# Starting the FFN on two batches of four in a fused retention and SwGLU kernel, and moving the next chunk's attention by a slot or two

## Chip, cores, metric

One core of one Trainium2 chip. The metric is the device time of one execution in microseconds (us). Several executions are timed for each kernel, the kernel before and the changed one in turn on the same chip. An execution is marked fast or slow; on one core "slow" only means that it took over 1.5% longer than the fastest of the same kernel.

## The reference

```python
# retention: q, k, v are (4 batches, 8 heads, 768 steps, 64)
state = gamma[None, :, None, None] * state + np.einsum('bhd,bhe->bhde', k[:, :, t], v[:, :, t])
y[:, :, t] = scale * np.einsum('bhd,bhde->bhe', q[:, :, t], state)
# then, on x = y as (4 * 768 tokens, 512):
xn = x / np.sqrt(np.mean(x * x, axis=-1, keepdims=True) + 1e-06) * rms_g
g = xn @ w_gate                                   # 512 x 1536
out = (g * (1.0 / (1.0 + np.exp(-g))) * (xn @ w_val)) @ w_out
```

All inputs and the output are float32; the kernel multiplies in bf16.

## The kernel before

It works in 6 chunks of 128 steps. The FFN of chunk c is a list of slots on TensorE: 12 for gate and value (one of 12 column blocks each, `gv`), then the output products (`down`). Pieces of the attention of chunk c+1, and the loads and transposes of chunk c+2, are hung onto these slots by number. I call the pieces of one batch V (v times decay), T (transposes of q and k), A (scores), Y (output, state update, sum of squares), R (rstd, one over the root of the mean square), N (norm) and X (transpose of the normed tile, giving xnT), S the first state; L is a load of q, k and v by GpSimd's queue. Chunks 0 and 1 transpose on TensorE; chunks 2 to 5 transpose by DMA, issued from SyncE's queue. In profile lines xn is a normed tile and xt_ps its transpose on TensorE, qT and kT are the transposed q and k, a_ps the scores, am the scores times decay or mask, g_ps and v_ps gate and value, hT their product, o_ps the output, and hot the zero tile of the filler.

```python
    # ahead of the FFN: H = filler matmuls on a zero tile, G and U = loads of gate and value weights
    for step in ("H9 H8 C0 T0 H4 V0 A0 H4 V1 T1 H4 G0 Y0 R0 U0 H4 A1 V2 T2 H4 Y1 R1 G1 U1 H2 A2 N0 T3 Y2 R2 "
                 "X0 N1 H2 A3 X1 N2 H9 H6 X2 H3 V3 Y3 H6 G2 U2 R3 N3").split():
        P[step[0]](0, int(step[1]))
    # ... cut: piece_t
        if c > 1:
            for n in "qk":
                t = work.tile([128, NHP, 128], BF16, name=n + "T", bufs=8)
                nc.sync.dma_start_transpose(out=t, in_=d[n + "b"])
                d[n + "T"] = t
            return
    # ... cut: in which slot of FFN c a piece of chunk c+1 stands, by batch
    PLAN = dict(a=(5, 5, 9, 9), y=(7, 8, 11, 12), n=(9, 10, 13, 13))
    PLAN1 = dict(v=(7, 9, 11, 14), t=(8, 10, 12, 15), a=(9, 11, 14, 17), y=(10, 13, 16, 19), n=(12, 15, 18, 21), x=(13, 17, 20, 22))
    # ... cut: loads (L) and transposes (T) for chunk c+2 (with -1: chunk c+1), W = output weights
    AHEAD = {1: ((L, 0),), 3: ((L, 1),), 5: ((L, 2),), 7: ((T, 0),), 8: ((T, 1),), 9: ((L, 3),), 11: ((T, 2),), ...}
    AHEAD0 = {2: ((L, -1, 1),), 4: ((W, 0),), 5: ((L, -1, 2),), 6: ((W, 1),), 8: ((L, -1, 3),), 9: ((W, 2), (L, 0)),
              11: ((L, 1),), 13: ((T, 0),), 14: ((L, 2),), 15: ((T, 1),), 19: ((T, 2), (L, 3))}
    LATE0 = {0: ((V, 0), (V, 1), (V, 2)), 1: ((T, 3),), 4: ((V, 3),)}    # in FFN 1, for chunk 2
```

## Time and profile before

| | before |
|---|---|
| time, median of the first 3 executions | 237.87 us (237.45 to 238.83) |
| span of the profiled execution | 236.0 us |
| TensorE (PE) busy | 226.4 us, 96% |
| mean granted PE clock | 0.998 |
| first FFN matmul | 20.43 us |

PE is full from 20.43 us on but for waits of 1.86 us in all. The lines that show this are in the prediction. Two more views also belong here, and I had not asked for either. The first is SyncE's queue between 45 and 95 us, here the rows around the DMA transposes of chunk 2, batches 2 and 3 (start, time in the queue, what):

```profile
58.81 1.19 SPq L183 DMA_TRANSPOSE qT<-qb  x1
60.52 1.19 SPq L183 DMA_TRANSPOSE kT<-kb  x1
61.81 1.52 SPq L381 DMA_DIRECT2D out_dram<-o_sb  x3
...
65.78 1.74 SPq L183 DMA_TRANSPOSE qT<-qb  x1
67.72 1.19 SPq L183 DMA_TRANSPOSE kT<-kb  x1
```

The rows at 58.81 and 60.52 are batch 2's, ahead of the output stores; those at 65.78 and 67.72 are batch 3's. The trace has batch 3's k landing at 67.70 and its kT at 74.72. PE wants kT near 81: the kernel before is 6.3 us ahead here.

The second is the DMA view of the stretch from 68 to 92 us:

```profile
DMA packets 14356, 3.96 MB, mean 165 GB/s; under 512 B 13851, under 2 KB 13851, under 8 KB 14354
q0 software_dynamic: 8653, 2.12, 113.6%
q1 hardware_dynamic: 5701, 1.81, 56.4%
```

q0 is GpSimd's queue (the loads), q1 SyncE's and ScalarE's (transposes, stores); the last figure of a row is the time that its packets took, over 16 engines' time; packets overlap, so it can pass 100%.

### The profile page before, as it was taken

Reading aid. Unit: us, or ns where it says so; the run is one execution under the profiler, and the core shown is the slowest. Engines: PE = TensorE matmul, PEld = TensorE weight load, DVE = VectorE, ACT = ScalarE, POOL = GpSimd, SP = SyncE. Lnnn points to the kernel's source line nnn. Section 1 sums busy time; section 2 is a strip of 40 time slices with the busy share of each in tenths; the row PEclk is TensorE's granted clock in tenths of the full one; section 3 lists DMA queues with packets and bytes.
Section 4 is the critical chain, followed back from the end, with each engine's and each line's share of the span. In section 5 each row is a group of like instructions: output and inputs, shape, how many; then the busy total and the mean of one; then the engine's idle time right before and its main releaser. Section 6 shows DMA issues by size and latency. Waiting matters only on the chain.

```text
span 236.0 us, 4231 instructions
## 1 busy us (share of the span) xinstructions
PE 226.4 (96%) x1587; PEld 119.3 (51%) x1613; DVE 126.8 (54%) x212; ACT 88.9 (38%) x172; POOL 128.5 (54%) x198
## 2 busy tenths in 40 slices
PE   7979999999899999999999999999999999999994
PEld 4657744565345555445554445554445554444443
DVE  6585435678337794147794147794148582243300
ACT  7475544432433423333433333433332532433221
POOL 8978989887997458970458970559300202000000
PEclk9999999999999999999999999999999999999999
DMA  7999999999999998899099999695900025200022
GB/s 135 178 188 204 211 193 204 206 196 139 180 271 174 163 139 152 172 213 161 11 127 122 173 205 104 79 133 135 181 0 0 3 44 152 73 0 0 0 89 90
DMA packets 87956, 30.69 MB, mean 130 GB/s; under 512 B 78528, under 2 KB 83392, under 8 KB 87936
## 3 DMA queue, kind: packets, MB, share of 16 engines
q0 software_dynamic: 54432, 16.78, 70.9%
q1 hardware_dynamic: 32832, 13.51, 30.7%
q8 instruction: 12, 0.20, 0.4%
q10 hardware_dynamic: 672, 0.13, 0.3%
q14 instruction: 8, 0.07, 0.1%
HBM read 28.58 MB, written 6.29 MB: 148 GB/s over the span
## 4 chain that ended last, share of the span: by engine, by line
PE 85%; DVE 4%; ACT 4%; POOL 3%; issue 2%; ACTq 0%; DVEq 0%; POOLq 0%
PE g_ps L340 26%; PE v_ps L340 26%; PE o_ps L375 21%; PE a_ps L208 3%; PE y_ps L226 2%; PE hot_ps L401 2%; PE y_ps L231 2%; PE kv_ps L257 2%; DVE am L214 1%; DVE xn L286 1%; PE o_ps L365 1%; ACT xsq L241 1%; DVE x L237 1%; PE xt_ps L296 1%; POOL rstd L274 1%
## 5 line engine op out<-in xcount | busy, mean ns | idle before, releaser
L344 DVE TENSOR_TENSOR hT<-sg,v_ps 128x512 bf16<-128x512 bf16 (+1 forms) x73 | 49.5, 678 | 79.9 <-PE v_ps L340 70.0
L340 PE MATMUL v_ps<-xnT,wv_b 128*128 128x512 bf16 (+2 forms) x298 | 73.5, 368 | 0.4
L340 PE MATMUL g_ps<-xnT,wg_b 128*128 128x512 bf16 (+2 forms) x293 | 73.1, 368 | 0.5
L343 ACT ACTIVATE sg<-g_ps 128x512 bf16<-128x512 f32 (+1 forms) x73 | 43.0, 589 | 64.8 <-PE g_ps L340 62.4
L375 PE MATMUL o_ps<-wo_b,hT 128*128 128x512 bf16 x267 | 61.9, 379 | 0.5 <-issue 0.2
L340 PEld LDWEIGHTS <-wv_b 128*128 128x128 bf16 x304 | 29.1, 98 | 33.1
L340 PEld LDWEIGHTS <-wg_b 128*128 128x128 bf16 x304 | 27.7, 98 | 29.2 <-DVE xnT L302 0.4
L375 PEld LDWEIGHTS <-hT 128*128 128x128 bf16 x276 | 26.1, 98 | 28.7 <-DVE hT L344 0.2
L271 POOL TENSOR_SCALAR ms<-ssq 128x1 f32<-128x1 f32 x24 | 5.6, 232 | 62.3 <-ACT xsq L241 61.9
L241 ACT ACTIVATE xsq<-x 128x512 f32<-128x512 f32 x20 | 12.6, 630 | 35.1 <-DVE x L237 33.3
L214 DVE TENSOR_TENSOR am<-a_ps,causal 128x512 bf16<-128x512 f32 x40 | 24.9, 679 | 0.0
L380 ACT COPY o_sb<-o_ps 128x512 f32<-128x512 f32 x23 | 13.2, 581 | 29.3 <-PE o_ps L375 23.3
L69 POOL DMA_DIRECT2D qb<-in_q_dram x23 | 21.7, 944 | 0.4 <-DMA kb<-in_k_dram 0.3
L175 POOL TENSOR_TENSOR vp<-v_f,vdec 128x512 bf16<-128x512 f32 x21 | 21.5, 1042 | 0.5
L74 POOL DMA_DIRECT2D v_f<-in_v_dram x23 | 21.3, 924 | 0.1
L69 POOL DMA_DIRECT2D kb<-in_k_dram x23 | 20.7, 901 | 0.1
L267 POOL CAST st_b<-st_f 64x256 bf16<-64x256 f32 x40 | 18.1, 454 | 1.3
L237 DVE TENSOR_TENSOR x<-y_ps,ydec 128x512 f32<-128x512 f32 x20 | 13.7, 684 | 2.9 <-PE y_ps L231 2.9
L282 DVE SCALAR_TENSOR_TENSOR xn<-x,rstd,g_bc 128x512 bf16<-128x512 f32 x16 | 12.7, 791 | 3.5 <-POOL rstd L274 3.5
L274 POOL TENSOR_TENSOR rstd<-ms,mhalf 128x1 f32<-128x1 f32 x24 | 13.3, 555 | 2.0
L401 PE MATMUL hot_ps<-hot 128*128 128x256 bf16 x65 | 11.6, 329 | 1.1 <-DVE hot L93 1.1
L226 PEld LDWEIGHTS <-am 128*128 128x128 bf16 x192 | 8.8, 98 | 5.3 <-DVE am L214 0.9
(71 smaller groups left out, 145.5 us busy)
## 6 DMA issues: line engine op xcount, KB each, us to landing
v_f<-in_v_dram POOLq DMA_DIRECT2D x23, 256.0 KB, 7.3
out_dram<-o_sb SPq DMA_DIRECT2D x23, 256.0 KB, 2.3
qb<-in_q_dram POOLq DMA_DIRECT2D x23, 128.0 KB, 7.1
kb<-in_k_dram POOLq DMA_DIRECT2D x23, 128.0 KB, 6.8
wo_b<-in_moe_w_out_dram POOLq DMA_DIRECT2D x3, 512.0 KB, 9.7
wg_b<-in_moe_w_gate_dram POOLq DMA_DIRECT2D x2, 384.0 KB, 6.5
wv_b<-in_moe_w_val_dram POOLq DMA_DIRECT2D x2, 384.0 KB, 7.3
wg_b<-in_moe_w_gate_dram POOLq DMA_DIRECT2D x1, 768.0 KB, 8.6
```

The source lines that it names most:

```text
L69: nc.gpsimd.dma_start(out=x.rearrange("p (h d) -> p h d", h=H), in_=src[b].rearrange("h (c p) d -> c p h d", p=C)[c])
L74: nc.gpsimd.dma_start(out=d["v_f"], in_=v[b].rearrange("h (c p) d -> c p h d", p=C)[c])
L175: (nc.vector if c == 0 and b < 3 else nc.gpsimd).tensor_tensor(out=d["vp"], in0=d["v_f"], in1=vdec[:, c, :, None].to_broadcast([128, H, D] ...
L214: nc.vector.tensor_tensor(out=am[:, i], in0=a_ps[i], in1=mask, op=ALU.mult)
L237: nc.vector.tensor_tensor(out=x, in0=y_ps, in1=ydec[:, c, :, None].to_broadcast([128, H, D]), op=ALU.mult)
L267: nc.gpsimd.tensor_copy(st_b[b][r, :, i * 64:i * 64 + 64], st_f[b][r, :, i * 64:i * 64 + 64])
L274: nc.gpsimd.tensor_tensor(out=rstd, in0=ms, in1=mhalf, op=ALU.pow)
L340: nc.tensor.matmul(ps[:, n - n0, :], w_b[:, s, n * 128:(n + 1) * 128], xnT[:, s, t], start=s == 0, stop=s == KS - 1)
L343: nc.scalar.activation(sg, g_ps, AF.Silu)
L344: nc.vector.tensor_tensor(out=hT[:, n0:n1, t], in0=sg, in1=v_ps, op=ALU.mult)
L375: nc.tensor.matmul(o_ps, hT[:, n, b * C:(b + 1) * C], wo_b[:, n, :], start=n == 0, stop=n == NFF - 1)
L401: nc.tensor.matmul(hot_ps, hot[:, 0:128], hot, start=True, stop=True)
```

## The change

Its intent: the FFN begins when two batches are ready instead of three, and the first weights are loaded ahead of the fourth batch, so less filler is run. The fourth batch's attention and the third's X go into the first slots. Chunk 1's pieces move one or two slots later, each batch's T ahead of the previous batch's Y and N, and X of its batch 3 goes into FFN 1.

```diff
-    WB = ((0, 384), (384, 768), (768, DFF))
+    WB = tuple((i * 384, (i + 1) * 384) for i in range(4))
-    PLAN1 = dict(v=(7, 9, 11, 14), t=(8, 10, 12, 15), a=(9, 11, 14, 17), y=(10, 13, 16, 19), n=(12, 15, 18, 21), x=(13, 17, 20, 22))
+    PLAN1 = dict(v=(9, 10, 13, 16), t=(9, 11, 13, 16), a=(10, 12, 15, 18), y=(11, 14, 17, 20),
+                 n=(13, 16, 19, 22), x=(15, 18, 21, None))
-        for b in range(B):
-            for n, slot in plan.items():
-                s[slot[b]].append(lambda f=pieces[n], b=b: f(c, b))
+        for n, slot in plan.items():
+            for b in range(B):
+                if slot[b] is not None:
+                    s[slot[b]].append(lambda f=pieces[n], b=b: f(c, b))
 (cut: gv takes a piece to run between its gate and value halves; load takes the names of what to load; of chunk 0's X
 only batch 0's is evicted by ScalarE, the others by VectorE; S casts its state as well, and its call moves into `first`;
 Y of chunk 0's batch 3 takes another PSUM pool; V of batch 3 stands last ahead of the FFN)
+        def first(i):                      # slots of FFN 0
+            two, three, third, fourth = slice(0, 2 * C), slice(0, 3 * C), slice(2 * C, 3 * C), slice(3 * C, GT)
+            if i == 0:
+                gv(0, 2, two, lambda: piece_x(0, 2))
+                gv(2, 3, two)
+                gv(0, 3, third)
+            elif i < 8:
+                gv(i + 2, t=three)
+            else:
+                gv(*((0, 4), (4, 8), (8, 10), (11, 12))[i - 8], fourth if i < 11 else slice(0, GT))
+                if i == 10:
+                    gv(10)
+            for f, *x in {1: ((piece_s, 0),), 2: ((piece_t, 0, 3), (piece_s, 1)), 3: ((piece_a, 0, 3),),
+                          4: ((piece_s, 2), (piece_y, 0, 3), (piece_rstd, 0, 3)), 5: ((piece_n, 0, 3), (piece_s, 3)),
+                          6: ((piece_x, 0, 3),)}.get(i, ()):
+                f(*x)
+        def second(n):                     # first two slots of FFN 1
+            gv(n, t=slice(0, GT - C))
+            if n == 0:
+                piece_x(1, B - 1)
+            else:
+                gv(0, 2, slice(GT - C, GT))
-    for step in (... "X0 N1 H2 A3 X1 N2 H9 H6 X2 H3 V3 Y3 H6 G2 U2 R3 N3").split():
+    for step in ("H9 H8 C0 T0 H4 V0 A0 H4 V1 T1 H4 G0 U0 Y0 G1 U1 R0 H4 A1 V2 T2 H4 q3 Y1 R1 k3 H2 A2 H6 N0 Y2 R2 v3 "
+                 "H2 X0 N1 H3 X1 N2 H6 G2 U2 G3 U3").split():
-    AHEAD0 = {2: ((L, -1, 1),), 4: ((W, 0),), 5: ((L, -1, 2),), 6: ((W, 1),), 8: ((L, -1, 3),), 9: ((W, 2), (L, 0)),
-              11: ((L, 1),), 13: ((T, 0),), 14: ((L, 2),), 15: ((T, 1),), 19: ((T, 2), (L, 3))}
+    AHEAD0 = {3: ((L, -1, 1),), 5: ((W, 0),), 6: ((L, -1, 2),), 8: ((W, 1),), 9: ((L, -1, 3),),
+              10: ((W, 2), (L, 0)), 12: ((L, 1),), 13: ((T, 0),), 15: ((T, 1),), 16: ((L, 2),), 20: ((L, 3),), 23: ((T, 2),)}
```

More of the change, by code (lines that the diff above doesn't have):

```diff
@@ L63, in load_first, with load @@
             raw[name] = x
-    def load(c, b):
+    def load(c, b, parts="qkv"):
         d = cur.setdefault((c, b), {})
-        for name, src in (("qb", q), ("kb", k)):
-            x = work.tile([128, DM], BF16, name=name, bufs=8)
-            nc.gpsimd.dma_start(
-                out=x.rearrange("p (h d) -> p h d", h=H),
-                in_=src[b].rearrange("h (c p) d -> c p h d", p=C)[c])
-            d[name] = x
-        d["v_f"] = loads.tile([128, H, D], F32, name="v_f")
-        nc.gpsimd.dma_start(out=d["v_f"], in_=v[b].rearrange("h (c p) d -> c p h d", p=C)[c])
+        for n in parts:
+            if n == "v":
+                x = d["v_f"] = loads.tile([128, H, D], F32, name="v_f")
+            else:
+                d[n + "b"] = work.tile([128, DM], BF16, name=n + "b", bufs=8)
+                x = d[n + "b"].rearrange("p (h d) -> p h d", h=H)
+            nc.gpsimd.dma_start(out=x, in_=dict(q=q, k=k, v=v)[n][b].rearrange("h (c p) d -> c p h d", p=C)[c])
     cur = {}
@@ L122 @@
     make_identity(nc, ident)
-    for b in range(1, B):
+    for b in (1, 2):
         load(0, b)
@@ L218, in piece_y @@
         d = cur[c, b]
-        pool, tag = (fps, "ff") if c == 0 else (aps, "at")
+        pool, tag = (fps, "ff") if c == 0 and b < B - 1 else (aps, "at")
         y_ps = pool.tile([128, H, D], F32, name="y_ps", tag=tag)
@@ L262, in piece_s @@
         nc.scalar.copy(st_f[b], piece_kv(0, b))
+        piece_sb(b)
     def piece_sb(b):
@@ L297, in piece_x @@
         xnT = cur[c, "xnT"][:, :, b * C:(b + 1) * C]
-        if c == 0 and b < 2:
+        if (c, b) == (0, 0):
             for s in range(KS):
@@ L329, in ffn, with gv @@
         slots = []
-        def gv(n0, n1=None, t=slice(0, GT)):
+        def gv(n0, n1=None, t=slice(0, GT), between=None):
             n1 = n0 + 1 if n1 is None else n1
@@ L337, in gv @@
             for ps, w_b in ((g_ps, wg_b), (v_ps, wv_b)):
+                if between is not None and ps is v_ps:
+                    between()
                 for n in range(n0, n1):
@@ L344, in gv @@
             nc.vector.tensor_tensor(out=hT[:, n0:n1, t], in0=sg, in1=v_ps, op=ALU.mult)
-        EARLY = 4
-        early = slice(0, GT - C)
-        def gv_first(n):
-            gv(n, t=early)
-            if n == 1:
-                piece_x(0, B - 1)
-            if n == EARLY - 1:
-                gv(0, EARLY, slice(GT - C, GT))
+        def first(i):
[18 more added lines that the diff above has]
+                piece_x(1, B - 1)
+            else:
+                gv(0, 2, slice(GT - C, GT))
         o_t = {}
@@ L383, in ffn @@
         for n in range(NFF):
-            slots.append(lambda n=n: gv_first(n) if c == 0 and n < EARLY else gv(n))
+            slots.append(lambda n=n: first(n) if c == 0 else second(n) if c == 1 and n < 2 else gv(n))
         if c == 0:
@@ L403 @@
     P = dict(C=lambda c, b: piece_c(b), V=piece_v, T=piece_t, A=piece_a, Y=piece_y,
-             R=piece_rstd, N=piece_n, X=piece_x, G=lambda c, i: load_wg(i), U=lambda c, i: load_wv(i), H=warm_up)
-    for step in ("H9 H8 C0 T0 H4 V0 A0 H4 V1 T1 H4 G0 Y0 R0 U0 H4 A1 V2 T2 H4 Y1 R1 G1 U1 H2 A2 N0 T3 Y2 R2 "
-                 "X0 N1 H2 A3 X1 N2 H9 H6 X2 H3 V3 Y3 H6 G2 U2 R3 N3").split():
+             R=piece_rstd, N=piece_n, X=piece_x, G=lambda c, i: load_wg(i), U=lambda c, i: load_wv(i), H=warm_up,
+             **{n: lambda c, b, n=n: load(c, b, n) for n in "qkv"})
+    for step in ("H9 H8 C0 T0 H4 V0 A0 H4 V1 T1 H4 G0 U0 Y0 G1 U1 R0 H4 A1 V2 T2 H4 q3 Y1 R1 k3 H2 A2 H6 N0 Y2 R2 v3 "
+                 "H2 X0 N1 H3 X1 N2 H6 G2 U2 G3 U3").split():
         P[step[0]](0, int(step[1]))
@@ L409 @@
     load(1, 0)
+    piece_v(0, 3)
     L, T, V, W = load, piece_t, piece_v, lambda c, i: load_wo(i)
@@ L435 @@
             f_slot()
-            if c == 0 and i < B:
-                piece_s(i)
-                piece_sb(i)
             for f in a_slots[i]:
```

## The prediction

> **What bounds the kernel now.** I read the page first: the engine shares, then the chain that ended last.
>
> ```profile
> PE 226.4 (96%) x1587; PEld 119.3 (51%) x1613; DVE 126.8 (54%) x212; ACT 88.9 (38%) x172; POOL 128.5 (54%) x198
> PE 85%; DVE 4%; ACT 4%; POOL 3%; issue 2%; ACTq 0%; DVEq 0%; POOLq 0%
> ```
>
> TensorE (PE) is busy for 96% of the span, and 85% of the chain is PE: the end is set by how much PE has to issue, plus the time in which it issues nothing useful. A busy PE can be issuing filler, so I next read the PE timeline of the first 21 us. Columns: start, length, engine, line, operation, tiles.
>
> ```profile
> 16.00 0.40 PE L296 MATMUL xt_ps<-ident,xn 128*128 128x128 bf16 x4 [0.28 <-DVE xn L286]
> 16.87 0.40 PE L296 MATMUL xt_ps<-ident,xn 128*128 128x128 bf16 x4
> 17.11 1.80 PE L401 MATMUL hot_ps<-hot 128*128 128x256 bf16 x15
> 18.98 0.40 PE L296 MATMUL xt_ps<-ident,xn 128*128 128x128 bf16 x4
> 19.21 0.49 PE L401 MATMUL hot_ps<-hot 128*128 128x256 bf16 x3
> 19.54 0.40 PE L226 MATMUL y_ps<-vp,am 128*128 128x64 bf16 x8
> 19.77 0.82 PE L401 MATMUL hot_ps<-hot 128*128 128x256 bf16 x6
> 20.43 0.81 PE L340 MATMUL g_ps<-xnT,wg_b 128*128 128x384 bf16 x4
> ```
>
> The three xt_ps rows are the transposes X0, X1, X2 of the first three batches (I write T, A, Y, N, X for the pieces of one batch and S for its state). Between 17.11 and 20.43 PE runs 24 matmuls on the zero tile hot: filler while it waits for the third batch. The FFN begins at 20.43. From there on I asked for PE's waits up to the end:
>
> ```profile
> PE xt_ps L296 <- DVE xn L286: 0.9, 1, 0.9
> PE a_ps L208 <- ACT qkT L198: 0.3, 1, 0.3
> ```
>
> Almost none. But an end of a matmul is modelled, so I also compared starts: a start minus the previous one, less the usual step for that width. This gives 0.44 us at 44.83 (A of chunk 1, batch 1), 0.29 at 47.64 (X of batch 0), about 0.1 at 54.45 and 1.03 at 60.49 (X of batch 3): 1.86 us in all, every one in chunk 1's attention. Steps of just 0.22 recur all through the trace; they are one missing 512-column record each and I don't count them. The largest wait, in the timeline of 57 to 63 us:
>
> ```profile
> 57.73 1.89 PE L375 MATMUL o_ps<-wo_b,hT 128*128 128x512 bf16 x8
> 60.49 0.40 PE L296 MATMUL xt_ps<-ident,xn 128*128 128x128 bf16 x4 [0.87 <-DVE xn L286]
> 61.67 1.04 PE L340 MATMUL g_ps<-xnT,wg_b 128*128 128x512 bf16 x3
> ```
>
> **What the Trainium skill says.** "TensorE: Matmul & The Clock Gate", Back-to-back issue gap, gives N/2.4 + 2.5 ns for a warm matmul of N columns. The trace agrees: four of 512 take 0.865 us from start to start (0.216 each), four of 384 take 0.65 (0.163), six of 256 take 0.66 (0.110), sixteen of 128 take 0.90 (0.056). So cutting a block by batches costs only some 3 ns for every matmul more. The same page (Part 1) says that an idle PE falls back to half clock after about 3.4 us; the trace starts slow (256 columns in 0.21 us until about 9 us) and shows no later fall. The change keeps filler in every gap, so I expect no loss of clock. "DMA: Bandwidth & Descriptors", Issuing engines are not separate DMA queues, says that all transfers share 16 engines and interleave. In the trace the loads that GpSimd issues land strictly one after the other: the last weight block, issued at 19.54, landed only at 31.48. So moving the weights ahead of batch 4 is a reordering of one full queue.
>
> **Part 1: FFN on two batches.** In the changed kernel PE's order ends X0, 3 fillers, X1, 6 fillers, FFN. From the VectorE (DVE) timeline of before: am of batch 2 ends at 15.28, N0 and N1 follow (1.40 us for both) and end at 16.60. X1's four transposes then run from 16.65; a DVE eviction of such a tile started 0.43 after the first transpose (18.98 to 19.41) and took 0.69, so X1's is done at about 17.8. X0's eviction on ScalarE (ACT) starts after xsq of batch 2, which no longer waits behind T3's copy: about 16.45 + 1.1 = 17.55. FFN starts at about 17.85 instead of 20.43: **-2.58 us**.
>
> What no longer stands before the FFN stands in it, on a full PE: T3 0.45 (8 transposes), A3 0.33, Y3 0.23, X2 0.22: **+1.23**. S0 to S3 and X3 were inside already.
>
> Widths, chunk 0. Before: 32 of 384, 32 of 128, 64 of 512 columns. After, from the listing of its instructions: 24 of 256, 24 + 80 of 128, 56 of 384, 16 of 512. By the four steps above, 20.85 and 21.0 us: **+0.15**.
>
> **Part 2: weights ahead of batch 4.** Landing times of before: v of batch 2 at 13.01, then some 1.95 us for each 384 KB weight block and 0.9 to 1.1 for a q, k or v. With the new order (two gate and two value blocks, then q, k, v of batch 3, then the other four) I get 14.9, 16.9, 18.8, 20.8, then 23.7 for the last of batch 3, then 25.7, 27.6, 29.6, 31.5. Needed: first blocks 17.85 and 18.9, second 22.0, T3 24.8, third gate 27.1 and value 27.8, fourth 32 and later. All in time, the third value block by 0.2 us only.
>
> **Part 3: batch 4 inside the block.** Here I charge new waits. FFN slots are 1.3 us (eight matmuls of 384) plus pieces: slot 0 ends at about 22.0, T3 is issued at 24.8, A3 at 26.8, Y3 at 28.65. ACT: qkT copy (1.01) from 25.5 to 26.4, a state copy to 26.9, silu to 27.4; DVE: that block's hT to 27.95, then the two am (1.29) to about 29.25. Y3 wants both: **+0.5**. Then xsq, and rstd on GpSimd (POOL), which by its order stands behind three DMA issues (0.9 each) and a cast (0.85): rstd at about 32.1, N3 (0.74) at 32.9, while PE reaches X3 at 32.3: **+0.6**.
>
> **Part 4: chunk 1.** Its pieces move one to two slots later, each T goes ahead of the previous batch's Y, and X of batch 3 goes into FFN 1's first slot, behind eight matmuls on three batches. The wait at 44.83 came because T's copy stood behind xsq on ACT (43.16, 43.78); now it stands ahead. X of batch 3 gains slot 23 (0.87) and the new first slot (1.3), more than 1.03. By following DVE, ACT and POOL through the slots I find all four waits gone: **-1.86**. One may replace them: rstd of batch 2 stands behind three DMA issues on POOL, as it did before at 53.09 to 55.92, and PE now reaches its X about as early as before, some 0.4 ahead of xn: **+0.4**. The split of two blocks of FFN 1 costs 0.03. Chunks 2 to 5 run as before.
>
> **Sum.** -2.58 + 1.23 + 0.15 + 0.5 + 0.6 - 1.86 + 0.4 + 0.03 = -1.5 us. The waits I charged are the pessimistic ends of hand-followed chains, so I put the middle slightly lower: 237.87 - 1.8 = **236.1 us**.
>
> **Rivals.** (a) The moved pieces cause no waits at all: without the 1.5 us charged, the gain is 3.0 and the time 234.9. For it: DVE is idle near half of the time between 20.4 and 42 (9.7 busy of 21.6), ACT likewise. Against: order, not load, makes these waits; each engine runs in order. (b) The weights become the bound: DMA is saturated up to about 90 us, and the third value block has 0.2 us of slack. If the early loads land 1 us later than I order them, PE waits 1 us or more at slot 4, though this partly covers Y3's wait: about 236.9. (c) PE reaches chunk 1 earlier but its loads, on the full queue, land as late as before, so that chunk 1's T, V or the output weights end the wait: the start's gain is given back and the time is 237 to 238. Against: q and k of its batch 0 land at 33.4 and are wanted at 38; the output weights land at 39.9 and are wanted at 44.
>
> **Range and chances.** All paths lie within 3 us of before, because only about 5 us of waits and filler exist to be removed. 2% is 4.8 us: more than the whole of rival (a), so faster by over 2% is nearly excluded, as is slower. The range, 235.0 to 237.3, goes from just above (a) to between (b) and (c); runs of before differ by 1.4 us, mostly one high value.
>
> **What would show each step.** FFN's first g_ps at 17.6 to 18.1 (part 1); no PE wait on wv_b or wg_b (part 2); waits of about half a microsecond at Y3 on am and at X3 on xn (part 3); between 42 and 62 no wait of a_ps on qkT and none over 0.5 at any xt_ps, and FFN 1's first matmul about 1.8 to 2 us earlier than 61.67 (part 4); from there on the same work at the same pace. I am wrong if FFN starts later than 18.5, if a weight wait over 0.5 stands near 27 us, or if chunk 1 shows a new wait over 1 us.

## The result

The changed kernel took 244.83 us (243.72 to 245.19, 4 executions) against 237.76 us (4 executions). The ratio is 1.0281 with a 95% interval of 1.0235 to 1.0327: slower. (A ratio is the mean time of one kernel's fast executions over that of the other's of the same rounds, so it is not quite the ratio of the medians.) The span of the profiled execution is 243.2 us.

From the page after the change, the engine and chain lines that answer to those of before:

```profile
PE 227.2 (93%) x1667; PEld 122.8 (50%) x1692; DVE 128.0 (53%) x216; ACT 88.5 (36%) x171; POOL 128.7 (53%) x200
PE 67%; POOL 15%; DMA 12%; issue 3%; DVE 1%; ACT 1%; POOLq 0%; ACTq 0%; DVEq 0%
```

PE has as much to do as before but a lower share, and the chain now runs for 27% of the span over GpSimd and DMA. PE's timeline around the start of the FFN:

```profile
15.89 0.40 PE L296 MATMUL xt_ps<-ident,xn 128*128 128x128 bf16 x4
16.55 0.40 PE L296 MATMUL xt_ps<-ident,xn 128*128 128x128 bf16 x4
16.78 0.82 PE L420 MATMUL hot_ps<-hot 128*128 128x256 bf16 x6
17.82 1.03 PE L344 MATMUL g_ps<-xnT,wg_b 128*128 128x256 bf16 x8 [0.22 <-DVE xnT L302]
```

The FFN starts at 17.82 instead of 20.43. PE's waits over the whole execution (total, times, longest), and PE's timeline at the longest of them:

```profile
PE a_ps L207 <- DMA kT<-kb: 5.3, 1, 5.3
PE xt_ps L296 <- DVE xn L286: 1.6, 2, 0.9
PE y_ps L225 <- DVE am L213: 0.7, 2, 0.4
```

```profile
80.60 0.40 PE L207 MATMUL a_ps<-qT,kT 64*128 64x128 bf16 x8
86.29 0.61 PE L207 MATMUL a_ps<-qT,kT 64*128 64x128 bf16 x8 [5.29 <-DMA kT<-kb]
86.83 1.89 PE L344 MATMUL g_ps<-xnT,wg_b 128*128 128x512 bf16 x4
```

The scores of chunk 2, batch 2 run at 80.60, those of batch 3 wait for their kT until 86.29. Then four matmuls of 512 columns stand for 1.89 us instead of 1.03. The view by stretches says why (columns: stretch, length, busy time of the five engines with their counts, granted PE clock, DMA share, GB/s):

```profile
80.90:86.20 5.30, 0.09 (x4) 0.00 (x0) 1.89 (x3) 0.29 (x1) 4.55 (x8) 0.83 1.90 91
86.20:91.40 5.20, 5.11 (x20) 1.97 (x21) 2.82 (x5) 0.60 (x1) 0.00 (x0) 0.51 1.84 144
91.40:100.00 8.60, 8.55 (x66) 4.65 (x66) 5.17 (x8) 3.21 (x7) 3.28 (x8) 1.00 1.41 179
```

PE stood idle, the granted clock fell to half at 84.42 and came back at 91.25, and DMA moved little while it was busy. In SyncE's queue batch 2's and 3's transposes now stand like this:

```profile
62.84 1.22 SPq L182 DMA_TRANSPOSE qT<-qb  x1
64.15 1.71 SPq L182 DMA_TRANSPOSE kT<-kb  x1
72.13 1.20 SPq L182 DMA_TRANSPOSE qT<-qb  x1
74.49 1.19 SPq L182 DMA_TRANSPOSE kT<-kb  x1
```

| chunk 2 | before: issued, landed | after: issued, landed |
|---|---|---|
| kT of batch 2 | 60.52, 64.54 (4.0) | 64.15, 76.16 (12.0) |
| k of batch 3 | 61.58, 67.70 (6.1) | 63.13, 74.47 (11.3) |
| kT of batch 3 | 67.72, 74.72 (7.0) | 74.49, 86.24 (11.8) |

Each transfer takes longer, and since a transpose is issued when its load has landed, the delays add up. The DMA view from 68 to 92 us:

```profile
DMA packets 11313, 2.84 MB, mean 118 GB/s; under 512 B 11056, under 2 KB 11056, under 8 KB 11312
q0 software_dynamic: 7925, 2.01, 162.0%
q1 hardware_dynamic: 3387, 0.81, 50.4%
```

Fewer bytes than before (2.84 against 3.96 MB), yet the packets took more time. Of the packets in this stretch 311 took over 0.45 us each; their times add up to 78% of the 16 engines' time (all packets: 213%). In the kernel before it was 151 and 34% (all: 171%). I call such a stretch a jam. From 30 to 50 us, where no DMA transpose is in flight, the kernel before had 11 such packets in 20 us, and moved 199 GB/s.

**The sum.** At the first scores of chunk 2 (71.67 against 72.14) the changed kernel is 0.47 us ahead. The wait costs 5.45 us by starts (a start minus the previous one, less the usual step). The half clock costs about 2.3: ten matmuls of 512 columns from 86.83 to 91.25 at 0.43 instead of 0.216 each, and eight scores. 236.0 - 0.47 + 5.45 + 2.3 = 243.3 against a span of 243.2.

### The profile page after: what moved, and what is told of

It is laid out like the page before. It is cut to its first block, busy times and chain, and to the rows that moved or that the text cites. A ratio compares the mean times of both kernels' runs of the same rounds, so it can differ in the third digit from the quotient of the medians.

```text
span 243.2 us, 4407 instructions
## 1 busy us (share of the span) xinstructions
PE 227.2 (93%) x1667; PEld 122.8 (50%) x1692; DVE 128.0 (53%) x216; ACT 88.5 (36%) x171; POOL 128.7 (53%) x200
## 4 chain that ended last, share of the span: by engine, by line
PE 67%; POOL 15%; DMA 12%; issue 3%; DVE 1%; ACT 1%; POOLq 0%; ACTq 0%; DVEq 0%
PE o_ps L394 20%; PE g_ps L344 20%; PE v_ps L344 19%; DMA kb<-in_k_dram 7%; DMA kT<-kb 5%; POOL qb L73 3%; POOL kb L73 3%; POOL v_f L73 2%; POOL st_b L267 2%; PE a_ps L207 2%; POOL vp L174 1%; PE y_ps L225 1%; PE y_ps L230 1%; POOL rstd L274 1%; PE o_ps L384 1%
## 5 line engine op out<-in xcount | busy, mean ns | idle before, releaser
L348 DVE TENSOR_TENSOR hT<-sg,v_ps 128x512 bf16<-128x512 bf16 (+2 forms) x76 | 50.0, 658 | 80.1 <-PE v_ps L344 69.1
L344 PE MATMUL g_ps<-xnT,wg_b 128*128 128x512 bf16 (+3 forms) x338 | 75.2, 346 | 0.7 <-DVE xnT L302 0.2
L344 PE MATMUL v_ps<-xnT,wv_b 128*128 128x512 bf16 (+3 forms) x343 | 75.0, 345 | 0.3
L347 ACT ACTIVATE sg<-g_ps 128x512 bf16<-128x512 f32 (+2 forms) x76 | 43.5, 573 | 75.4 <-PE g_ps L344 70.5
L344 PEld LDWEIGHTS <-wv_b 128*128 128x128 bf16 x348 | 31.9, 98 | 31.5 <-issue 1.3
L344 PEld LDWEIGHTS <-wg_b 128*128 128x128 bf16 x348 | 30.5, 99 | 28.3 <-issue 2.5
L267 POOL CAST st_b<-st_f 64x256 bf16<-64x256 f32 x40 | 17.2, 429 | 1.9 <-ACT st_f L261 0.7
L248 DVE TENSOR_TENSOR st_f<-st_f,kv_ps 128x512 f32<-128x512 f32 x16 | 10.8, 676 | 0.0
```

Of the source, the lines that this page charges most:

```text
L267: nc.gpsimd.tensor_copy(st_b[b][r, :, i * 64:i * 64 + 64], st_f[b][r, :, i * 64:i * 64 + 64])
L344: nc.tensor.matmul(ps[:, n - n0, :], w_b[:, s, n * 128:(n + 1) * 128], xnT[:, s, t], start=s == 0, stop=s == KS - 1)
L347: nc.scalar.activation(sg, g_ps, AF.Silu)
L348: nc.vector.tensor_tensor(out=hT[:, n0:n1, t], in0=sg, in1=v_ps, op=ALU.mult)
```

## The experiments

First the theory: T of chunk 2, batch 2, moved behind the stores, runs together with the loads of batch 3; that delays these and with them batch 3's own T. The rival: chunk 1's new order makes all loads of chunk 2 late, and the place of T does not matter. All runs gave correct results.

**e1: T of batch 2 back in slot 19.**

```diff
-    10: ((W, 2), (L, 0)), ..., 16: ((L, 2),), 20: ((L, 3),), 23: ((T, 2),)}
+    10: ((W, 2), (L, 0)), ..., 16: ((L, 2),), 19: ((T, 2),), 20: ((L, 3),)}
```

> The changed kernel, with one entry put back: the DMA transposes of q and k of chunk 2, batch 2 are issued in slot 19, ahead of the four output stores and of the gain broadcast, instead of in slot 23 behind them. Theory A (those transposes, moved late, run into the loads of batch 3, which makes those loads late, and so batch 3's own transposes): the PE wait of 5.3 us for kT at 86.29 shrinks to under 1 us, no stretch at half clock, time 237.0 to 238.0. Theory B (the loads of chunk 2 are later as a whole by the new order of chunk 1, the place of the transposes does not matter): wait of over 4 us stays, time 243 to 245.

236.97 us (236.71 to 237.65) against 237.53, ratio 0.9976 (0.9955 to 0.9997). The long wait is gone; 0.4 us of it is left in the view of the profiled execution, 0.6 by starts:

```profile
PE a_ps L207 <- DMA kT<-kb: 0.4, 1, 0.4
```

Here kT of batch 3 landed at 81.38, 9.75 us after its issue. So undoing the one move removes most of the loss, but not because transfers are now as early as in the kernel before (74.72). This kernel ran in four executions on one chip and was not run again.

**e2: that move alone, in the kernel before** (`19: ((T, 2), (L, 3))` becomes `19: ((L, 3),), 23: ((T, 2),)`).

> The kernel before, with only that one entry moved as the change moves it: transposes of chunk 2, batch 2 from slot 19 to slot 23. Theory A: the wait for kT of batch 3 appears in it, 3 to 6 us near 81 us[...]; time 241 to 246. Theory B: as before, 237.5 to 238.3.

237.86 us (237.46 to 238.03), ratio 1.0004: no effect. kT of batch 3 landed at 77.47 instead of 74.72, still ahead of its need. The theory as I stated it fails: the late T is not enough by itself. Of the rival, e1 refutes that the place of T does not matter; that chunk 1's new order makes the transfers of chunk 2 late may still be so. What is left is that both are needed: something else in the change uses up most of the 6.3 us. (These landings are of one profile each; e3 shows how far they vary.)

**e3: 40 filler matmuls ahead of batch 3's scores.**

```diff
+        if (c, b) == (2, 3):
+            for _ in range(40):
+                nc.tensor.matmul(a_ps[0][:, 0:2, :], hot[:, 0:128], hot, start=True, stop=True)
```

> The changed kernel, with 40 matmuls of 256 columns on the zero tile (about 4.4 us) put ahead of the scores of chunk 2, batch 3, so that PE is not idle while it waits; the wait itself stays. If the granted clock fell because of the idle time, and cost what it seems (4.95 us at half speed after the wait ended, so some 2.5 us): granted clock 0.998 instead of 0.986 and time 242.0 to 242.8 against 244.8. If the clock's fall has another cause or costs nothing: time as the changed kernel's or longer.

241.71 us (241.31 to 241.97), granted clock 1.0 (the trace holds no clock record; four matmuls of 512 columns step in 0.86 us, as at full clock elsewhere). The time is just under the expected 242.0 to 242.8, but I cannot use it: in the profiled execution kT of batch 3 landed at 79.78, ahead of need, so these 241.7 us may as well be a kernel without a wait plus 4.4 us of filler. The run showed something else: with the same instructions up to that point the transfers landed 6.5 us apart from the changed kernel's profile.

**e4: chunk 3's loads and transposes later**, from slots 1, 3, 5, 7, ... of FFN 1 to 7, 8, 10, 11, ...

```diff
+    AHEAD1 = {7: ((L, 0),), 8: ((L, 1),), 10: ((L, 2),), 11: ((T, 0),), 12: ((L, 3), (T, 1)), 13: ((V, 0),),
+              14: ((V, 1), (T, 2)), 15: ((V, 2), (V, 3), (T, 3))}
-        for f, *x in (AHEAD0 if c == 0 else AHEAD).get(i, ()) ...
+        for f, *x in (AHEAD0 if c == 0 else AHEAD1 if c == 1 else AHEAD).get(i, ()) ...
```

> The changed kernel, transposes left in slot 23, but the loads and transposes of chunk 3 (which in FFN 1 begin in slots 1, 3, 5 and 7) begin in slots 7, 8, 10 and 11, so that they are not in the queues while chunk 2, batch 3 is transposed. Theory A2 (transposes and loads in flight together slow each other): batch 3's q and k transposes land within 6 us of their issue instead of 11.8, wait at the scores under 1 us, time 237 to 239 unless chunk 3 now comes late and makes a wait of its own. Theory B: the transposes are issued at 72 and still take over 10 us, the wait stays over 4 us.

The part that was to be told apart came out as theory A2 has it: kT of batch 3 took 2.4 us from issue to landing (73.27 to 75.67; the last load beside it landed at 74.06), and the wait at the scores is gone. But k of batch 3 still took 10.5 us (62.77 to 73.25), so chunk 3's loads are not what slows that load. The time did not: 247.91 us (247.72 to 248.25). Chunk 3's loads now met the transposes of chunk 2's normed tiles (xnT), and the same jam came back in front of FFN 2:

```profile
PE g_ps L344 <- DMA xnT<-xn: 8.7, 1, 8.7
```

I had named a late chunk 3 as the risk; it was chunk 2's xnT.

**e5: the kernel before with the chunk 1 part alone** (the new PLAN1, order, AHEAD0 and `second`; start as before).

> The kernel before, with only the chunk 1 part of the change (its slots, the order of its pieces, its loads, X of batch 3 in FFN 1's first slot, and the late transposes of chunk 2, batch 2); the start of the FFN is as before. Theory C (the wait needs the two together: chunk 1's new slots use up the 6.3 us by which batch 3's kT was early in the kernel before, and the late transposes then add some 5 us): the wait for kT of chunk 2, batch 3 is there, 2 to 6 us, time 239 to 245. If the earlier start of the FFN is needed for it: no such wait, time 236 to 237.5, since the waits of chunk 1 (1.86 us) are gone.

241.58 us (238.51 to 243.05, 6 executions), ratio of the fast ones 1.0155 (1.0126 to 1.0184). The wait is there, in the shortest execution, which is the profiled one (2.2 us by starts):

```profile
PE a_ps L208 <- DMA kT<-kb: 2.1, 1, 2.1
```

So theory C holds: it needs the chunk 1 part, with the late T, and not the earlier start.

**e6 and e12: the changed kernel again**, on chips 7 and 9 (e1 to e4 ran on chip 0).

> The changed kernel once more, unedited, to see whether the wait is the same in another execution and on this chip. In the run with filler the same loads and transposes, with the same instructions ahead of them, landed 6.5 us earlier (kT of batch 3 at 79.78 against 86.24). If the transfers' pace is a matter of each execution: a wait of another length, between 0 and 6 us, and a time between 238 and 245. If it is fixed by the program: 5 to 5.6 us and 244 to 245.5 again.

> The changed kernel a third time, unedited, beside the others on one chip. Its fast runs so far: 243.7 to 245.2 on one chip, 238.2 to 241.8 on another. If the wait's length is a matter of each execution: again a spread of 2 us or more within 238 to 245. If it was set by the chip of the first runs: near one value.

e6: 239.48, 241.78, 242.79 and 238.23 us; ratio of the fast ones 1.0079 (1.0006 to 1.0152). e12: 241.46, 240.55, 238.14, 238.59, 238.50 and 239.10 us; ratio 1.0069 (1.0028 to 1.011). The wait at the scores was 2.3 us in e6's profile (kT landed at 83.22, the scores began at 83.27) and 3.05 in e12's. So its length is a matter of each execution, and 2.8% is the bad end of a range. Whether the four long executions of the first result came from its chip or from chance, I cannot say.

**e11: the start alone** (PLAN1, order, AHEAD0 and FFN 1 as in the kernel before).

> The changed kernel with the chunk 1 part taken back (slots, order, loads and transposes as in the kernel before), so that only the start of the FFN is changed. By the sum of what the traces show: 2.6 us earlier start, less 1.23 us of moved pieces, 0.15 for widths, 0.43 at Y and 0.95 at X of batch 3, so within 0.3 us of the kernel before: 237.3 to 238.0. If chunk 1's old slots wait more now that the FFN comes to them otherwise: 238 to 239.5. No wait for kT over 1 us in either case.

238.58 us (238.49 to 238.91) against 237.59, ratio 1.0039 (1.0015 to 1.0063): a loss of 1 us, even, without a wait for kT. The miss is chunk 1: X of its batch 0 now waits 1.11 us (0.29 before). The start gives nothing by itself.

**e7 and e9: loads split so that rstd comes first.** In the changed kernel two X pieces wait for a norm, the norm for rstd, and rstd on GpSimd stands behind three DMA issues. GpSimd's timeline of the changed kernel at the second one:

```profile
54.64 0.97 POOL L73 DMA_DIRECT2D qb<-in_q_dram  x1
55.61 0.89 POOL L73 DMA_DIRECT2D kb<-in_k_dram  x1
56.48 0.92 POOL L73 DMA_DIRECT2D v_f<-in_v_dram  x1
57.47 0.19 POOL L271 TENSOR_SCALAR ms<-ssq 128x1 f32<-128x1 f32 x1
57.74 0.56 POOL L274 TENSOR_TENSOR rstd<-ms,mhalf 128x1 f32<-128x1 f32 x1
```

The edit, with T of batch 2 in slot 19 (Q, K, F load q, k, v alone; J loads k and v):

```diff
-    AHEAD0 = {3: ((L, -1, 1),), ...                                   16: ((L, 2),), 20: ((L, 3),), 23: ((T, 2),)}
+    AHEAD0 = {3: ((Q, -1, 1), (K, -1, 1)), 4: ((F, -1, 1),), ...      16: ((Q, 2),), 17: ((J, 2),), 19: ((T, 2),), 20: ((L, 3),)}
```

> The changed kernel with the early transposes (slot 19), and with two loads split so that a norm's rstd no longer stands behind three DMA issues on GpSimd: q and k of chunk 1, batch 1 stay in slot 3, v goes behind rstd of batch 3; q of chunk 2, batch 2 stays in slot 16, k and v go behind rstd of chunk 1, batch 2. If these issues are what the two xt_ps waits of 0.95 and 1.03 us come from: both fall to under 0.3, time 235.0 to 236.0 against 236.97 of the early transposes alone. Rival: k of chunk 2, batch 2 lands later and its transposes run into the next loads again, and a wait for kT of 1 us or more eats the gain: 236 to 240.

> The kernel with early transposes and split loads once more, unedited, with more rounds and beside the changed kernel on one chip. It had kT of chunk 2, batch 3 landed at 76.9, some 2.6 us ahead of need, and one run of four at 236.73. If that slack is enough: 234.6 to 235.2 in nearly all runs, at most one in six over 236. If the pace of the transfers on another chip uses it up: a median of 235.5 to 238.

e7: 234.86, 234.85, 234.85 and 236.73 us, ratio 0.989 (0.9847 to 0.9932); both waits at xt_ps are gone from the profile. This seemed the better kernel. e9, the same on another chip: 243.89, 236.38, 235.24, 240.19, 242.50 and 241.26 us, a median of 240.7 and so outside both expectations. Its profiled execution, a long one, has no wait at the scores; it waits 5.7 us at 100.36 for xnT, which landed at 100.27. One run of four executions had hidden that.

**e10: scores of batch 3 one slot later**, on top of e7 (`a=(5, 5, 9, 10)` for chunk 2).

> The same with the scores of chunk 2, batch 3 one slot later (10 instead of 9; its output stays in slot 12), which gives its kT 1.73 us more. If kT is what the rare long runs wait for: no run over 235.8, median 234.6 to 235.2 as without it. If the later scores cause a wait of their own (am for the output, or the next norm): 235.2 to 236.5.

235.32, 243.35, 244.29, 235.03, 243.30 and 242.25 us: a miss: no execution over 235.8 was expected, and four are. So more time for kT does not help. The profiled execution is a short one; what the long ones waited for is not on record (in e9 and e15 it is xnT).

**e8: T of chunk 2, batches 2 and 3 on TensorE**, else as the changed kernel.

```diff
-        if c > 1:
+        if c > 1 and not (c == 2 and b in (2, 3)):
-    LATE0 = {0: ((V, 0), (V, 1), (V, 2)), 1: ((T, 3),), 4: ((V, 3),)}
+    LATE0 = {0: ((V, 0), (V, 1), (V, 2)), 3: ((T, 2),), 4: ((V, 3),), 7: ((T, 3),)}
 (cut: T of batch 2 leaves slot 23 of FFN 0)
```

> The changed kernel, with q and k of chunk 2, batches 2 and 3 transposed by TensorE (16 transposes, 0.9 us, and two ScalarE copies of 1.0 us) instead of by DMA, so that four DMA transposes are out of the queues while loads are in flight. If transposes in flight are what slows the loads: qb and kb of batch 3 land within 7 us of issue (9.9 and 11.3 in the changed kernel), no PE wait at the scores, granted clock 0.998, time 237.3 to 238.5 (237.3 without the wait, plus 0.9, less what is hidden). If loads are slow for another reason, they take over 9 us still.

238.46 us (238.29 to 238.69), ratio 1.0022 (0.9998 to 1.0047), no wait at the scores. q, k and v of batch 3 landed 7.0, 6.5 and 6.5 us after issue, against 9.9, 11.3 and 11.8. The loads behind them took 3.6 to 5.9 us. The four executions lie within 0.4 us.

**e13, e14: the same with the split loads; e15, e16: with and without it on one chip.** e13 is e7 with both T on TensorE, e14 and e16 with batch 2's alone (`(c, b) != (2, 2)`, in slot 3 of FFN 1), e15 is e7 unedited.

> The kernel with the split loads, with q and k of chunk 2, batches 2 and 3 transposed by TensorE instead of by DMA. If DMA transposes in flight with loads are what makes the long executions: all six runs within 0.8 us of each other, none with granted clock under 0.995, and 235.4 to 236.6 (234.85 of the good runs without it, plus 16 transposes or 0.9 us, less or more a wait of up to 0.5 for a weight block). If the long executions have another cause: some runs of 239 or more again.

> The same with batch 2 alone on TensorE (8 transposes, 0.45 us); batch 3 stays with the DMA. If batch 2's transposes, in flight with batch 3's loads, are enough to start the jam: runs as even as those with both on TensorE and 235.0 to 236.0. If batch 3's transposes jam with chunk 3's loads by themselves: some runs of 238 or more.

> The kernel with split loads and all of chunk 2's transposes on the DMA, unedited, on the same chip as the next one. If the transposes' place makes the difference and not the chip: a spread of 2 us or more again, at least two of six runs over 236.5 with a lower granted clock in the longest. If the chip does: all runs within 234.6 to 235.3.

> The kernel with batch 2's transposes of chunk 2 on TensorE, unedited, on the same chip as the one before. If the place of those transposes makes the difference: all runs within 0.8 us, 235.3 to 236.1. If it was the chip: runs of 238 or more whenever the other has them.

| | T of chunk 2, batches 2 and 3 | executions, us | ratio of fast ones |
|---|---|---|---|
| e13 | both on TensorE | 236.03 to 236.62 (6) | 0.9938 (0.9922 to 0.9953) |
| e14 | 2 on TensorE, 3 by DMA | 235.44 to 235.95 (6) | 0.9912 (0.9898 to 0.9926) |
| e15 | both by DMA | 243.49, 235.23, 244.78, 243.19, 242.21, 243.80 | one fast execution: none |
| e16 | 2 on TensorE, 3 by DMA | 235.51 to 235.99 (4) | 0.9916 (0.9902 to 0.9930) |

e15 and e16 ran in turn on one chip and differ only in where and when batch 2's q and k are transposed. PE's waits of e15 in a long execution:

```profile
PE g_ps L344 <- DMA xnT<-xn: 5.9, 1, 5.9
```

e15's long executions are over 1.5% longer than its fast one. Their granted clock is 0.984 to 0.991. In the profiled one this is what the wait leaves behind: the half clock begins at 98.37, inside the wait, and lasts 6.8 us. That it is so in the other four is not shown. Therefore I compare the spread, 9.6 against 0.5 us, and no ratio. e14, which is 2.1 us faster than the kernel before by the mean of its fast executions, is the version that beats both.

e7 and e15 are the same program on chip 7: in one launch no execution was over 236.8 us, in the other five of six were over 242. So the chip alone does not decide whether it jams.

## Why the prediction was wrong

- **Part 1, the earlier start, was right.** 17.82 measured, 17.85 predicted. That it is so close is partly luck: over all runs with this start the FFN begins at 17.43 to 18.06.
- **Part 2, the weights, was right.** No wait on a weight in the changed kernel. The third value block landed at 27.13 (27.6 predicted). e8, in another execution, did wait 0.5 us for it: rival (b) was close.
- **Part 3 was right in mechanism**: Y of batch 3 waited 0.43 us for am (0.5 predicted) and X 0.93 for xn (0.6).
- **Part 4 was right for chunk 1's old waits, and too small in its one new term.** The old waits left the list, but X of batch 2 waited 1.03 us where I charged 0.4. With part 3's 0.33 this is most of the difference between the predicted 1.5 us and the 0.47 us that the changed kernel had won at chunk 2's scores. By the signs that the prediction named (no wait over 0.5 us at any xt_ps, FFN 1 earlier by 1.8 to 2 us) this part was off: 1.03 us, and 0.72 us (60.95 against 61.67). e7 shows both terms to be rstd behind DMA issues: with the loads split both waits vanish.
- **The step that failed is one sentence: "Chunks 2 to 5 run as before."** The moved entry, T of batch 2, stands in the diff; the prediction does not mention it, and has no step that asks when chunk 2's transfers land. The wait for kT (5.45 us) and the half clock behind it (2.3 us) are 7.75 us that no term of the sum held. Without them the span would be about 235.5 us. Times are some 1.7 us above spans here (244.9 and 243.2), so that is a time of about 237.2 us: just inside the range of 235.0 to 237.3, at its upper end and not at the middle of 236.1, because of part 4.
- **"All paths lie within 3 us of before" followed from counting only waits that exist.** A change can make a new one of any length. I kept rival (c), late loads, to chunk 1 and to load times; the transposes of chunk 2, in the same full queues, were not in it.
- **I expected no loss of clock, since the change keeps filler in the gaps.** That holds for the start alone; the new wait has no filler.

What is shown: the loss in the first result is the wait for kT and the half clock behind it. The wait is in the profiles of the changed kernel and of e5, which have both the chunk 1 part and the late T, is absent where the chunk 1 part is missing (e2, e11), and all but gone with T early (e1, one launch of four executions). But an early T is no cure: with the loads split too, T is early and the jam stands in front of xnT instead (e9, e15). With batch 2's transposes, or those of both batches, off the DMA queues it stays away by the times: all 20 executions lie within 0.6 us of the shortest of their run (e8, e13, e14, e16), and e16 ran in turn with e15, where five of six were long. Not shown is why loads and transposes slow each other as they do, whether it is the transposes themselves or the room that they leave, nor why some executions jam and others do not with the same instructions.

## What to carry to other kernels

Slack belongs to each transfer: before moving an issue by some slots, look up when its data landed, when it was wanted, and what will be in the queues beside it. A kernel whose engines are tuned to the last wait may sit at the edge of a DMA jam; time it in several executions, in several launches and on more than one chip, because one run of four can look 1.1% faster and the next have executions over 2% slower. And a wait on TensorE of 3.05 to 8.8 us (e12, the changed kernel, e9, e15, e4) cost, here, its own length and then some 1.7 to 2.9 us more in clock: an estimate, half of the 3.4 to 5.7 us that PE ran at half clock after the wait.

## What the Trainium skill lacked or had wrong

- "DMA: Bandwidth & Descriptors", DMA Transpose (X-bar), gives constraints and a warning of corruption, but no timing of transposes in flight with loads of another queue. Here one 128 x 512 bf16 transpose took 2.4 us from issue to landing with hardly a load beside it (e4) and 11.8 us with them (after); from 68 to 92 us the engines moved 118 GB/s instead of 165, with 311 packets of over 0.45 us instead of 151.
- "TensorE: Matmul & The Clock Gate", Part 1, has half clock after one idle window of about 3.4 us (its table under "Why this matters for your kernels", which warns of gaps over about 3 us, fits better). Here waits of 2.2 and 2.3 us (e5, e6) did not lower the clock, 3.05 us already did (e12, half clock for 3.4 us), 5.45 us did for 6.8 us: the stretches at half clock are whole multiples of 3.413 us, but the wait need not last a whole window. In e12 the clock fell at 84.49; of the 3.413 us before, PE was idle for about 2.5 and busy again for 0.94.
- The same page, Back-to-back issue gap, also gives 131 ns for a sustained stream of 512-column matmuls with their weight loads, and 81 ns for 128 columns. This kernel's steady stream of such pairs shows 216 and 56 ns, which is what the page calls the isolated gap.
